# Natural-layout dO by a transposing DMA instead of TensorE, in a two-block attention backward kernel

## The chip, the cores and the metric

The kernel runs on one core of a Trainium2 chip. The metric is device time in microseconds (us) of the whole program: the median of three runs of the kernel before is 1736.88 us (1735.48 to 1741.37). A core has TensorE (PE; its weight loads stand apart as PEld), VectorE (DVE), ScalarE (ACT), GpSimd (POOL) and SyncE (SP), which does no arithmetic here and issues most DMAs. All DMAs run on the core's 16 DMA engines.

## The reference

Two attention blocks, A and B, each with its own x, cached K and V, wq and wo, work side by side; their outputs are concatenated. The kernel returns the forward output and the gradients of everything, for a given `grad_out`.

```python
B, Sq, D = 8, 96, 640
H, Sk, Dh = 32, 512, 128
def block(x, k_cache, v_cache, wq, wo):
    q = (x @ wq).reshape(B, Sq, H, Dh).transpose(0, 2, 1, 3)
    scores = einsum("bhqd,bhkd->bhqk", q, k_cache) * Dh ** -0.5
    p = softmax(scores)
    o = einsum("bhqk,bhkd->bhqd", p, v_cache)
    return o.transpose(0, 2, 1, 3).reshape(B, Sq, H * Dh) @ wo
out = concatenate([block(A...), block(B...)], axis=-1)
out, vjp = jax.vjp(f, ...);  grads = vjp(grad_out)     # all in bfloat16
```

So each block yields out (8x96x640), dx, dK and dV (8x32x512x128 each), dwq (640x4096) and dwo (4096x640). In each head, with g the block's half of `grad_out`: Q = x wq_h, dO = g wo_h^T, P = softmax(QK^T), dV = P^T dO, dP = dO V^T, dS = P (dP - rowsum(O dO)), dK = dS^T Q, dQ = dS K.

## The kernel before

**Unit of work.** An item is one head h and one batch b: 96 query rows against 512 keys. A block has 32 heads of 8 items, so there are 64 heads and 512 items in all. They run through a software pipeline in ticks: item (h, b) of the block that begins at tick0 enters at tick `tick0 + 8h + b`, and stage s of it is emitted at that tick plus `OFF[s]` (line 45): load at 0, transposes of K and V at 2 (`c_s1`), scores and softmax at 3, transposes of P at 4 and O^T at 5 (`c_s45`), dV at 4 (`c_s4`), dP, delta and dS at 6 (`c_s6`), transposes of dS and dK at 7 (`c_s7`, `c_s78`), dQ^T at 8. Within a tick the slots of `SLOTS` (line 50) set the order. Block B follows block A without a break. The framework's scheduler may still reorder by its own priorities; it inserts the waits and gives out the buffers of the tile pools (`bufs` of them for each name or tag).

**Work of a head.** `HK` (line 46) gives the ticks of what is done once a head, from the tick of its item b = 0:

- `pA` loads wq_h (POOL queue) and `pV` loads wo_h transposed, by a transposing DMA on SP's queue; `pB` takes the tiles QT_h and dOT_h.
- `pC` (line 192) makes Q^T and dO^T, each in two halves of four batches, by matmuls over the five 128-chunks of D, evicted by ScalarE or VectorE. Both have the head's 128 columns on partitions and the queries along the free dimension. QT_h is padded to 128 queries a batch, its pad set to zero by POOL (line 181); dOT_h is not padded.
- dK and dV need Q and dO the other way round, queries on partitions ("natural"). For Q this is `pN` (line 227): one transposing DMA of QT_h into Qnat_h, issued on SP at tick -1. For dO it is `pD` (line 213): eight TensorE transposes (line 223) in two halves, at ticks 2 and 7, and a VectorE copy of each half out of PSUM into dOnat_h (line 157, in `evac`).
- `pW` loads wq_h transposed (wqT_h, transposing DMA on SP, tick 2). `qA` (line 409) turns O^T and dQ^T into natural layout (Onat at tick 13, dQnat at 16), again by transposing DMAs on SP. `qB` and `qD` make dwo and dwq from them.
- So each head issues five transposing DMAs on SP: wo, wq, Q, O and dQ.

**Work of a group.** Out and dx are summed over groups of eight heads (`gU`, line 468): 24 more matmuls a head on average, spread over the 26 ticks after a group has ended. In the first eight heads there are none yet.

**Queues.** SP issues in one order, from one queue, each item's K and V load (lines 238 and 239), its dV and dK store (lines 340 and 406), 128 KB each, and the head's five transposes. A DMA instruction whose data or buffer isn't ready holds up all those behind it. POOL issues the loads of wq and wo rows and the stores of dwo, dwq and (block A) out and dx; it also scales P (line 295) and multiplies O by dO (line 349). K_sb has 11 buffers, V_sb 8, dK_sb and dV_sb 5 each, P_sb 5.

**Setup of a block.** x and g must be transposed for `pC`. Block A does it from its natural copies; block B, while A's last heads run, loads column chunks of 128 (`setup_ld`, line 91, ten DMAs on the POOL queue) and transposes each chunk on TensorE (`setup_cT`, line 100).

Of the kernel before, what the change touches and what calls it, by code (L numbers as in the profile page):

```python
# [8 lines left out]
ALU = mybir.AluOpType  # L9
AX = mybir.AxisListType  # L10
F32 = mybir.dt.float32
BF16 = mybir.dt.bfloat16
# [18 lines left out]
SL_LOAD = 0  # L31
# [9 lines left out]
SL_HEAD = 90  # L41
SL_GRP = 95
SL_SETUP = 96

OFF = dict(ld=0, s1=2, s2=3, s3=3, s4=4, s5=5, s6=6, s7=7, s8=8)
HK = dict(pA=-6, pB=-4, pV=-5, pW=2, pC0=[-3, -2], pC1=[0, 1], pD1=[2, 7], pN=-1, qA0=13, qA1=16, qB=[18, 19], qD=[(20, 0, 3), (23, 3, 5)])
# [6 lines left out]
def build_block(tc, em, tick0, blk, x, kc, vc, wq, wo, g_all, out_all, dx, dk, dv, dwq, dwo, ident, ones, pools, HG=8, first=True):  # L53
    nc = tc.nc
# [28 lines left out]
    def bank(shape, dt, name):  # L83
        return ps.tile(shape, dt, name=name, tag="bank")

    S = {}
# [1 line left out]
    HS = pools["HS"]  # L88
    CS = pools["CS"]

    def setup_ld(which_, c):
        def f():
            tmp = const.tile([128, TT, 128], BF16, name="ld_tmp", bufs=3)
            src_flat = x_flat if which_ == 0 else g_flat
            with nc.allow_non_contiguous_dma(reason="setup column chunk"):
                tc.keep_in_program_order(nc.gpsimd.dma_start(tmp[:], src_flat[:, c * 128:(c + 1) * 128].rearrange("(t p) d -> p t d", p=128)))
            S[("tmp", which_, c)] = tmp
        return f

    def setup_cT(which_, c):  # L100
        def f():
            key = "xT" if which_ == 0 else "gT"
            if c == 0:
                S[key] = const.tile([128, DC, T], BF16, name=key, bufs=1)
            tmp = S.pop(("tmp", which_, c))
            pt = bank([128, TT, 128], BF16, "tp_ps")
            for t in range(TT):
                nc.tensor.transpose(pt[:, t, :], tmp[:, t, :], ident[:])
            nc.vector.tensor_copy(S[key][:, c, :], pt[:].rearrange("p t d -> p (t d)"))
        return f  # L110

    def setup_T(which_, t):
# [21 lines left out]
    if first:  # L134
        assert TT % 2 == 0
        for t in range(TT):
            if t % 2 == 0:
                em.add(tick0 - 12, SL_LOAD, setup_nat(0, t, 2))
                em.add(tick0 - 11, SL_LOAD, setup_nat(1, t, 2))
            em.add(tick0 - 10 + t // 2, SL_SETUP, setup_T(0, t))  # L140
            em.add(tick0 - 7 + t // 2, SL_SETUP, setup_T(1, t))
    else:
        for c in range(DC):
            em.add(tick0 - 12 + c + (c >= 3), SL_LOAD, setup_ld(0, c))
            em.add(tick0 - 9 + c, SL_SETUP, setup_cT(0, c))
            em.add(tick0 - 7 + c, SL_SETUP + 1, setup_ld(1, c))
            em.add(tick0 - 5 + c, SL_SETUP, setup_cT(1, c))
    if not first:
        em.add(tick0 + B + OFF["s5"] - 2, SL_LOAD, setup_nat(1))
        em.add(tick0 + B + OFF["s8"] - 2, SL_LOAD, setup_nat(0))  # L150
# [26 lines left out]
    def pB(h):  # L177
        def f():
            st = HS[(blk, h)]
            st["QT_h"] = hd.tile([128, B, 128], BF16, name="QT_h")  # L180
            nc.gpsimd.memset(st["QT_h"][:, :, Sq:128], 0.0)
            st["dOT_h"] = hd.tile([128, T], BF16, name="dOT_h")
        return f

    def pW(h):
# [6 lines left out]
    def pC(h, which, si):  # L192
        def f():
            st = HS[(blk, h)]
            (t0, w) = tsplits[si]
            b0 = t0 // Sq
            if which == 0:
                dst = st["QT_h"][:, b0:b0 + w // Sq, 0:Sq]
                lhs = lambda c: st["wq_h"][:, c, :]
                rhsT = S["xT"]  # L200
                sc = scale
            else:
                dst = st["dOT_h"][:, t0:t0 + w].rearrange("p (b q) -> p b q", q=Sq)
                lhs = lambda c: st["woT_h"][:, c, :]
                rhsT = S["gT"]
                sc = None
            q_ps = bank([128, w], F32, "q_ps")
            for c in range(DC):
                nc.tensor.matmul(q_ps[:], lhs(c), rhsT[:, c, t0:t0 + w], start=(c == 0), stop=(c == DC - 1))  # L209
            evac(EV["pC%d%d" % (which, si)], dst, q_ps[:].rearrange("p (b q) -> p b q", q=Sq), sc)  # L210
        return f

    def pD(h, half):
        def f():
            st = HS[(blk, h)]
            if half == 0:
                st["dOnat_h"] = hd.tile([Sq, B * 128], BF16, name="dOnat_h")
            b0 = half * HB
            nb = B - b0 if half else HB
            n_ps = bank([Sq, 8 * 128], BF16, "n_ps")  # L220
            for i in range(nb):
                b = b0 + i
                nc.tensor.transpose(n_ps[:, i * 128:(i + 1) * 128], st["dOT_h"][:, b * Sq:(b + 1) * Sq], ident[:])  # L223
            evac("dve", st["dOnat_h"][:, b0 * 128:(b0 + nb) * 128], n_ps[:, 0:nb * 128])
        return f

    def pN(h):
        def f():
            st = HS[(blk, h)]
            st["Qnat_h"] = hd.tile([128, B, 128], BF16, name="Qnat_h")  # L230
            tc.keep_in_program_order(nc.sync.dma_start_transpose(st["Qnat_h"][:], st["QT_h"][:].rearrange("p b q -> p (b q)")))
        return f

    def c_ld(h, b):
# [95 lines left out]
    def c_s4(h, b):  # L330
        def f():
            st = CS[(blk, h, b)]
            hs = HS[(blk, h)]
            P_sb = st["P_sb"]
            dV_ps = bank([128, KC * 128], F32, "dV_ps")
            for c in range(KC):
                nc.tensor.matmul(dV_ps[:, c * 128:(c + 1) * 128], P_sb[:, c * 128:(c + 1) * 128], hs["dOnat_h"][:, b * 128:(b + 1) * 128], start=True, stop=True)  # L337
            dV_sb = wk.tile([128, KC * 128], BF16, name="dV_sb", bufs=5)
            nc.scalar.activation(dV_sb[:], dV_ps[:], ACT.Identity, scale=1.0)  # L339
            nc.sync.dma_start(dv[b, h].rearrange("(p c) d -> p (c d)", c=KC), dV_sb[:])  # L340
        return f

    def c_s5b(h, b):
        def f():
            st = CS[(blk, h, b)]
            hs = HS[(blk, h)]
            tok = slice(b * Sq, (b + 1) * Sq)
            prod = wk.tile([128, Sq], BF16, name="prod", bufs=3)
            nc.gpsimd.tensor_tensor(prod[:], hs["OT_h"][:, tok], hs["dOT_h"][:, tok], op=ALU.mult)  # L349
            st["prod"] = prod  # L350
        return f

    def c_s6(h, b):
        def f():
            st = CS[(blk, h, b)]
            hs = HS[(blk, h)]
            tok = slice(b * Sq, (b + 1) * Sq)
            dP_ps = bank([Sq, Sk], F32, "dP_ps")
            nc.tensor.matmul(dP_ps[:], hs["dOT_h"][:, tok], st["VT"], start=True, stop=True)  # L359
# [58 lines left out]
    def qB(h, di):  # L418
        def f():
            st = HS[(blk, h)]  # L420
            Onat = st["Onat"]
            if "dwo_sb" not in st:
                st["dwo_sb"] = hd.tile([128, D], BF16, name="dwo_sb")
                st["dwo_n"] = 0
            dwo_sb = st["dwo_sb"]
            (c0, w) = dsplits[di]
# [9 lines left out]
    def qD(h, c_lo, c_hi):  # L436
        def f():
            st = HS[(blk, h)]
            dQnat = st["dQnat"]
            if "dwq_sb" not in st:  # L440
                st["dwq_sb"] = hd.tile([128, DC, 128], BF16, name="dwq_sb")
                st["dwq_n"] = 0
            dwq_sb = st["dwq_sb"]
            ncn = c_hi - c_lo
# [1 line left out]
            for ci in range(ncn):  # L446
                c = c_lo + ci
                for t in range(TT):
                    nc.tensor.matmul(w_ps[:, ci * 128:(ci + 1) * 128], S["x_nat"][:, t, c * 128:(c + 1) * 128], dQnat[:, t, :],  # L449
                                     start=(t == 0), stop=(t == TT - 1))  # L450
            evac("act" if ncn > 1 else "dve", dwq_sb[:, c_lo:c_hi, :].rearrange("p a b -> p (a b)"), w_ps[:, 0:ncn * 128])
            st["dwq_n"] += ncn
            if st["dwq_n"] == DC:
                with nc.allow_non_contiguous_dma(reason="per-head dwq slice"):
                    nc.gpsimd.dma_start(dwq_v[:, :, h * 128:(h + 1) * 128], dwq_sb[:])
        return f

    def gW(g, hh):
# [38 lines left out]
    for h in range(H):  # L497
# [1 line left out]
        em.add(c0t + HK["pA"], SL_LOAD, pA(h))  # L499
        em.add(c0t + HK["pB"], SL_HEAD, pB(h))  # L500
        em.add(c0t + HK["pV"], SL_HEAD, pV(h))
        em.add(c0t + HK["pN"], SL_HEAD + 0.5, pN(h))
        em.add(c0t + HK["pW"], SL_HEAD, pW(h))
        for si in range(NTS):
            em.add(c0t + HK["pC0"][min(si, len(HK["pC0"]) - 1)], SL_HEAD, pC(h, 0, si))
            em.add(c0t + HK["pC1"][min(si, len(HK["pC1"]) - 1)], SL_HEAD, pC(h, 1, si))
        for half in range(2):
            em.add(c0t + HK["pD1"][half], SL_HEAD, pD(h, half))
        for b in range(B):
            ct = c0t + b  # L510
            em.add(ct + OFF["ld"], SLOTS["LOAD"], c_ld(h, b))
# [142 lines left out]
```

## Time and profile before

One execution was profiled: 1739.57 us, of which its span (first to last recorded instruction) is 1737.8 us. The engine rows count arithmetic only; DMA-issuing instructions are not counted as busy, so SP has no such row and its load must be read from the timeline of its queue.

| view | before |
|---|---|
| span / time of the profiled run | 1737.8 / 1739.57 us |
| TensorE clock granted | 1.00 |
| DMA moved | 387.46 MB, mean 223 GB/s |
| DMA packets under 512 B | 294560 of 573454 |
| HBM read / written | 161.09 / 159.12 MB |
| SP's issues | 2079 copies, 320 transposes |
| copies dV, dK, K, V | 512 each, 128 KB, 3.2 to 3.4 us to landing |
| transposes Qnat_h, Onat, dQnat | 64 each, 4.5, 4.2 and 3.7 us to landing |
| transposes woT_h, wqT_h | 64 each, 3.7 to 3.8 us to landing |
| POOL memset of QT_h | 64 of 311 ns |

How to read it: times are us unless marked ns. A group's row gives line, engine, operation and tile (out<-in), then total busy time and mean length of one, then the engine's idle time just before. Matmuls are pipelined: the length of one (219 ns for 128 columns) is not the distance to the next (56 ns). A wait's row reads: who waited, for whom, us in total, how often, longest. A row of a time window gives its bounds, its length, the busy time and count on PE, PEld, DVE, ACT and POOL, then the granted clock, the DMA engines' busy share and GB/s. A row of a queue's timeline gives start, length, and what was issued.

### The profile page before, as it was taken

Reading aid. Unit: us, or ns where it says so; the run is one execution under the profiler, and the core shown is the slowest. Engines: PE = TensorE matmul, PEld = TensorE weight load, DVE = VectorE, ACT = ScalarE, POOL = GpSimd, SP = SyncE. Lnnn points to the kernel's source line nnn. Section 1 sums busy time; section 2 is a strip of 40 time slices with the busy share of each in tenths; the row PEclk is TensorE's granted clock in tenths of the full one; section 3 lists DMA queues with packets and bytes.
Section 4 is the critical chain, followed back from the end, with each engine's and each line's share of the span. In section 5 each row is a group of like instructions: output and inputs, shape, how many; then the busy total and the mean of one; then the engine's idle time right before and its main releaser. Section 6 shows DMA issues by size and latency. Waiting matters only on the chain.

```text
span 1737.8 us, 64947 instructions
## 1 busy us (share of the span) xinstructions
PE 1717.4 (99%) x24056; PEld 1441.5 (83%) x24056; DVE 1410.6 (81%) x2943; ACT 1476.5 (85%) x4081; POOL 767.5 (44%) x1385
## 2 busy tenths in 40 slices
PE   8999999999999999999999999999999999999998
PEld 6877888888888888888888888888888888888886
DVE  7877777888888888888887888778888888888885
ACT  6988888988889888888777999888888888888883
POOL 3444433444434444445455544344443444444441
PEclk9999999999999999999999999999999999999999
DMA  9998999989899988899999989999899989888994
GB/s 226 219 226 222 226 230 215 231 231 221 224 215 222 224 227 213 218 228 235 250 241 247 231 224 224 225 222 228 232 223 212 213 228 228 223 217 224 230 218 123
DMA packets 573454, 387.46 MB, mean 223 GB/s; under 512 B 294560, under 2 KB 561696, under 8 KB 573136
## 3 DMA queue, kind: packets, MB, share of 16 engines
q1 hardware_dynamic: 556656, 335.62, 80.3%
q0 software_dynamic: 16480, 47.70, 10.4%
q8 instruction: 188, 3.08, 0.8%
q14 instruction: 130, 1.06, 0.3%
HBM read 161.09 MB, written 159.12 MB: 184 GB/s over the span
## 4 chain that ended last, share of the span: by engine, by line
PE 96%; DMA 2%; DVE 0%; ACT 0%; issue 0%; POOL 0%; SPq 0%; DVEq 0%; POOLq 0%; ACTq 0%
PE q_ps L209 12%; PE o_ps L483 12%; PE kvT_ps L250 6%; PE dK_ps L403 6%; PE dV_ps L337 6%; PE kvT_ps L248 6%; PE dP_ps L359 6%; PE S_ps L264 6%; PE dwq_ps L449 6%; PE dwo_ps L429 6%; PE dq_dst_ps L386 5%; PE optp_ps L320 5%; PE optp_ps L311 5%; PE dq_dst_ps L377 5%; PE n_ps L223 2%; DMA woT_h<-in_A_wo_dram 1%
## 5 line engine op out<-in xcount | busy, mean ns | idle before, releaser
L295 POOL TENSOR_SCALAR P_sb<-E_sb,rinv 96x512 bf16<-96x512 bf16 x512 | 352.2, 688 | 638.5 <-DVE rinv L286 635.2
L363 DVE SCALAR_TENSOR_TENSOR dS_sb<-dP_ps,dl_ps,P_sb 96x512 bf16<-96x512 f32 x512 | 384.7, 751 | 102.1 <-PE dl_ps L361 88.3
L276 ACT ACTIVATE E_sb<-S_ps,negm 96x512 bf16<-96x512 f32 x512 | 348.6, 681 | 124.5 <-DVE negm L266 124.0
L266 DVE TENSOR_REDUCE negm<-S_ps 96x1 f32<-96x512 f32 x512 | 348.2, 680 | 68.3 <-PE S_ps L264 67.7
L252 DVE COPY KVT<-kvT_ps 128x1024 bf16<-128x1024 bf16 x512 | 349.4, 682 | 41.1 <-PE kvT_ps L250 24.2
L405 ACT ACTIVATE dK_sb<-dK_ps 128x512 bf16<-128x512 f32 x512 | 301.6, 589 | 56.4 <-PE dK_ps L403 53.2
L339 ACT ACTIVATE dV_sb<-dV_ps 128x512 bf16<-128x512 f32 x512 | 316.0, 617 | 0.0
L326 ACT ACTIVATE PT_sb<-optp_ps 128x384 bf16<-128x384 bf16 x512 | 254.7, 497 | 0.0
L349 POOL TENSOR_TENSOR prod<-OT_h,dOT_h 128x96 bf16<-128x96 bf16 x512 | 186.9, 365 | 106.5 <-ACT OT_h L323 87.6
L250 PE MATMUL kvT_ps<-ident,V_sb 128*128 128x128 bf16 x2048 | 197.9, 219 | 2.0 <-DMA V_sb<-in_A_v_cache_dram 2.0
L248 PE MATMUL kvT_ps<-ident,K_sb 128*128 128x128 bf16 x2048 | 197.9, 219 | 0.8 <-DMA K_sb<-in_A_k_cache_dram 0.8
L337 PE MATMUL dV_ps<-dOnat_h,P_sb 96*128 96x128 bf16 x2048 | 197.9, 219 | 0.0
L403 PE MATMUL dK_ps<-Qnat_h,dS_sb 96*128 96x128 bf16 x2048 | 197.9, 219 | 0.0
L264 PE MATMUL S_ps<-KVT,QT_h 128*96 128x512 bf16 x512 | 193.7, 378 | 1.6 <-DVE KVT L252 1.5
L359 PE MATMUL dP_ps<-KVT,dOT_h 128*96 128x512 bf16 x512 | 195.2, 381 | 0.0
L248 PEld LDWEIGHTS <-K_sb 128*128 128x128 bf16 x2048 | 152.9, 98 | 41.9 <-issue 1.7
L388 DVE COPY dST_sb<-dq_dst_ps 128x384 bf16<-128x384 bf16 x512 | 178.9, 349 | 2.9 <-PE dq_dst_ps L386 1.8
L386 PE MATMUL dq_dst_ps<-ident,dS_sb 96*128 96x96 bf16 x2048 | 172.1, 206 | 1.1 <-DVE dS_sb L363 1.0
L320 PE MATMUL optp_ps<-ident,P_sb 96*128 96x96 bf16 x2048 | 171.6, 205 | 1.5 <-POOL P_sb L295 1.5
L311 PE MATMUL optp_ps<-PT_sb,V_sb 128*128 128x96 bf16 x2048 | 172.1, 206 | 0.0
L377 PE MATMUL dq_dst_ps<-dST_sb,K_sb 128*128 128x96 bf16 x2048 | 170.8, 206 | 0.0
L449 PE MATMUL dwq_ps<-dQnat,x_nat 128*128 128x128 bf16 x1920 | 142.6, 219 | 3.5 <-DMA dQnat<-dQT_h 3.3
(70 smaller groups left out, 3475.0 us busy)
## 6 DMA issues: line engine op xcount, KB each, us to landing
out_dram<-dV_sb SPq DMA_DIRECT2D x512, 128.0 KB, 3.3
out_dram<-dK_sb SPq DMA_DIRECT2D x512, 128.0 KB, 3.2
K_sb<-in_A_k_cache_dram SPq DMA_DIRECT2D x256, 128.0 KB, 3.4
V_sb<-in_A_v_cache_dram SPq DMA_DIRECT2D x256, 128.0 KB, 3.4
K_sb<-in_B_k_cache_dram SPq DMA_DIRECT2D x256, 128.0 KB, 3.4
V_sb<-in_B_v_cache_dram SPq DMA_DIRECT2D x256, 128.0 KB, 3.3
out_dram<-dwo_sb POOLq DMA_DIRECT2D x64, 160.0 KB, 3.5
out_dram<-dwq_sb POOLq DMA_DIRECT2D x64, 160.0 KB, 4.6
```

The costliest lines, as they stand in the source:

```text
L248: nc.tensor.transpose(kvT_ps[:, c * 128:(c + 1) * 128], st["K_sb"][:, c, :], ident[:])
L250: nc.tensor.transpose(kvT_ps[:, Sk + c * 128:Sk + (c + 1) * 128], st["V_sb"][:, c, :], ident[:])
L252: nc.vector.tensor_copy(KVT[:], kvT_ps[:])
L266: nc.vector.tensor_reduce(negm[:], S_ps[:], axis=AX.X, op=ALU.max, negate=True)
L276: nc.scalar.activation(E_sb[:], st["S_ps"][:], ACT.Exp, bias=st["negm"][:], scale=1.0, accum_out=rowsum[:])
L295: nc.gpsimd.tensor_scalar(P_sb[:], st["E_sb"][:], st["rinv"][:], 0.0, op0=ALU.mult, op1=ALU.add)
L337: nc.tensor.matmul(dV_ps[:, c * 128:(c + 1) * 128], P_sb[:, c * 128:(c + 1) * 128], hs["dOnat_h"][:, b * 128:(b + 1) * 128], start=True, s ...
L339: nc.scalar.activation(dV_sb[:], dV_ps[:], ACT.Identity, scale=1.0)
L359: nc.tensor.matmul(dP_ps[:], hs["dOT_h"][:, tok], st["VT"], start=True, stop=True)
L363: nc.vector.scalar_tensor_tensor(dS_sb[:], dP_ps[:], dl_ps[:, 0:1], st["P_sb"][:], op0=ALU.subtract, op1=ALU.mult)
L403: nc.tensor.matmul(dK_ps[:, c * 128:(c + 1) * 128], dS_sb[:, c * 128:(c + 1) * 128], hs["Qnat_h"][0:Sq, b, :], start=True, stop=True)
L405: nc.scalar.activation(dK_sb[:], dK_ps[:], ACT.Identity, scale=1.0)
```

## The change

Natural dO now comes, like natural Q, from a transposing DMA on SP's queue, but only from the ninth head of block A on and in all of block B; in the first eight heads of block A both natural Q and natural dO are made by TensorE transposes. For this dOT_h takes QT_h's padded form and its pad is set to zero by POOL. dV moves from the item's tick 4 to its tick 6 (transposes of P stay at 4). The wqT transpose moves from tick 2 to 6 of the head, that of O from 13 to 12. Block B loads its x and g by six row chunks each (1280 contiguous bytes a row) instead of five column chunks (256 bytes). The row tiles, dwo_sb and dwq_sb share six buffers (before: 3, 2 and 2), and dV_sb has six buffers instead of five. Qnat_h and dOnat_h now have the same shape.

```diff
-OFF = dict(ld=0, s1=2, s2=3, s3=3, s4=4, s5=5, s6=6, s7=7, s8=8)
-HK = dict(pA=-6, pB=-4, pV=-5, pW=2, pC0=[-3, -2], pC1=[0, 1], pD1=[2, 7], pN=-1, qA0=13, qA1=16, ...)
+OFF = dict(ld=0, s1=2, s2=3, s3=3, s4=4, sv=6, s5=5, s6=6, s7=7, s8=8)
+HK = dict(pA=-6, pB=-4, pV=-5, pW=6, pC0=[-3, -2], pC1=[0, 1], pD1=[2, 7], pD0=[3, 6], pN=[-1, 1], qA0=12, qA1=16, ...)
...
+    def row640(name):
+        return hd.tile([128, D], BF16, name=name, tag="row640", bufs=6)
+
-    def setup_ld(which_, c):
-            tmp = const.tile([128, TT, 128], BF16, name="ld_tmp", bufs=3)
-            ... nc.gpsimd.dma_start(tmp[:], src_flat[:, c * 128:(c + 1) * 128].rearrange("(t p) d -> p t d", p=128))
+    def setup_ld(which_, t):
+            tmp = row640("ld_tmp")
+            ... nc.gpsimd.dma_start(tmp[:], src_flat[t * 128:(t + 1) * 128, :])
...
-            pt = bank([128, TT, 128], BF16, "tp_ps")
-            for t in range(TT):
-                nc.tensor.transpose(pt[:, t, :], tmp[:, t, :], ident[:])
-            nc.vector.tensor_copy(S[key][:, c, :], pt[:].rearrange("p t d -> p (t d)"))
+            pt = bank([128, DC, 128], BF16, "tp_ps")
+            for c in range(DC):
+                nc.tensor.transpose(pt[:, c, :], tmp[:, c * 128:(c + 1) * 128], ident[:])
+            nc.vector.tensor_copy(S[key][:, :, t * 128:(t + 1) * 128], pt[:])
...
-        for c in range(DC):
-            em.add(tick0 - 12 + c + (c >= 3), SL_LOAD, setup_ld(0, c))
-            em.add(tick0 - 9 + c, SL_SETUP, setup_cT(0, c))
-            em.add(tick0 - 7 + c, SL_SETUP + 1, setup_ld(1, c))
-            em.add(tick0 - 5 + c, SL_SETUP, setup_cT(1, c))
+        for t in range(TT):
+            em.add(tick0 - 11 + t, SL_LOAD, setup_ld(0, t))
+            em.add(tick0 - 9 + t, SL_SETUP, setup_cT(0, t))
+            em.add(tick0 - 8 + t, SL_LOAD, setup_ld(1, t))
+            em.add(tick0 - 6 + t, SL_SETUP, setup_cT(1, t))
...
     def pB(h):
-            nc.gpsimd.memset(st["QT_h"][:, :, Sq:128], 0.0)
-            st["dOT_h"] = hd.tile([128, T], BF16, name="dOT_h")
+            st["dOT_h"] = hd.tile([128, B, 128], BF16, name="dOT_h")
+            for k in range(2):
+                if BYDMA[k](h):
+                    nc.gpsimd.memset(st["dOT_h" if k else "QT_h"][:, :, Sq:128], 0.0)
...
-    def pD(h, half):
+    BYDMA = [lambda h: not first or h >= 8, lambda h: not first or h >= 8]
+    def pD(h, which, half):
...
+            src = st["dOT_h" if which else "QT_h"]
+            name = "dOnat_h" if which else "Qnat_h"
...
-                nc.tensor.transpose(n_ps[:, i * 128:(i + 1) * 128], st["dOT_h"][:, b * Sq:(b + 1) * Sq], ident[:])
+                nc.tensor.transpose(n_ps[:, i * 128:(i + 1) * 128], src[:, b0 + i, 0:Sq], ident[:])
...
-    def pN(h):
+    def pN(h, which):
...
+            src = st["dOT_h" if which else "QT_h"]
+            name = "dOnat_h" if which else "Qnat_h"
+            st[name] = hd.tile([128, B, 128], BF16, name=name)
+            tc.keep_in_program_order(nc.sync.dma_start_transpose(st[name][:], src[:].rearrange("p b q -> p (b q)")))
...
-            dV_sb = wk.tile([128, KC * 128], BF16, name="dV_sb", bufs=5)
+            dV_sb = wk.tile([128, KC * 128], BF16, name="dV_sb", bufs=6)
...
-                st["dwo_sb"] = hd.tile([128, D], BF16, name="dwo_sb")
+                st["dwo_sb"] = row640("dwo_sb")
...
-                st["dwq_sb"] = hd.tile([128, DC, 128], BF16, name="dwq_sb")
+                st["dwq_sb"] = row640("dwq_sb")
...
-        em.add(c0t + HK["pN"], SL_HEAD + 0.5, pN(h))
+        for k in range(2):
+            if BYDMA[k](h):
+                em.add(c0t + HK["pN"][k], SL_HEAD + 0.5, pN(h, k))
...
         for half in range(2):
-            em.add(c0t + HK["pD1"][half], SL_HEAD, pD(h, half))
+            for k in range(2):
+                if not BYDMA[k](h):
+                    em.add(c0t + HK["pD1" if k else "pD0"][half], SL_HEAD, pD(h, k, half))
...
-            em.add(ct + OFF["s4"], SLOTS["S4"], c_s4(h, b))
+            em.add(ct + OFF["sv"], SLOTS["S4"], c_s4(h, b))
```

More of the change, by code (lines that the diff above doesn't have):

```diff
@@ L43 @@
 SL_SETUP = 96
-OFF = dict(ld=0, s1=2, s2=3, s3=3, s4=4, s5=5, s6=6, s7=7, s8=8)
-HK = dict(pA=-6, pB=-4, pV=-5, pW=2, pC0=[-3, -2], pC1=[0, 1], pD1=[2, 7], pN=-1, qA0=13, qA1=16, qB=[18, 19], qD=[(20, 0, 3), (23, 3, 5)])
+OFF = dict(ld=0, s1=2, s2=3, s3=3, s4=4, sv=6, s5=5, s6=6, s7=7, s8=8)
+HK = dict(pA=-6, pB=-4, pV=-5, pW=6, pC0=[-3, -2], pC1=[0, 1], pD1=[2, 7], pD0=[3, 6], pN=[-1, 1], qA0=12, qA1=16, qB=[18, 19], qD=[(20, 0, 3), (23, 3, 5)])
 EV = dict(pB0="act", pB1="dve", pC00="act", pC01="act", pC10="act", pC11="dve", pD0="dve", pD1="dve", qA0="dve", qA1="dve", qB0="act", qB1="act", gU="act")
@@ L89, in build_block, with setup_cT @@
     CS = pools["CS"]
-    def setup_ld(which_, c):
+    def row640(name):
+        return hd.tile([128, D], BF16, name=name, tag="row640", bufs=6)
+    def setup_ld(which_, t):
         def f():
-            tmp = const.tile([128, TT, 128], BF16, name="ld_tmp", bufs=3)
+            tmp = row640("ld_tmp")
             src_flat = x_flat if which_ == 0 else g_flat
-            with nc.allow_non_contiguous_dma(reason="setup column chunk"):
-                tc.keep_in_program_order(nc.gpsimd.dma_start(tmp[:], src_flat[:, c * 128:(c + 1) * 128].rearrange("(t p) d -> p t d", p=128)))
-            S[("tmp", which_, c)] = tmp
+            tc.keep_in_program_order(nc.gpsimd.dma_start(tmp[:], src_flat[t * 128:(t + 1) * 128, :]))
+            S[("tmp", which_, t)] = tmp
         return f
-    def setup_cT(which_, c):
+    def setup_cT(which_, t):
         def f():
             key = "xT" if which_ == 0 else "gT"
-            if c == 0:
+            if t == 0:
                 S[key] = const.tile([128, DC, T], BF16, name=key, bufs=1)
-            tmp = S.pop(("tmp", which_, c))
-            pt = bank([128, TT, 128], BF16, "tp_ps")
-            for t in range(TT):
-                nc.tensor.transpose(pt[:, t, :], tmp[:, t, :], ident[:])
-            nc.vector.tensor_copy(S[key][:, c, :], pt[:].rearrange("p t d -> p (t d)"))
+            tmp = S.pop(("tmp", which_, t))
+            pt = bank([128, DC, 128], BF16, "tp_ps")
+            for c in range(DC):
+                nc.tensor.transpose(pt[:, c, :], tmp[:, c * 128:(c + 1) * 128], ident[:])
+            nc.vector.tensor_copy(S[key][:, :, t * 128:(t + 1) * 128], pt[:])
         return f
@@ L202, in f @@
             else:
-                dst = st["dOT_h"][:, t0:t0 + w].rearrange("p (b q) -> p b q", q=Sq)
+                dst = st["dOT_h"][:, b0:b0 + w // Sq, 0:Sq]
                 lhs = lambda c: st["woT_h"][:, c, :]
@@ L211, in pC @@
         return f
-    def pD(h, half):
+    BYDMA = [lambda h: not first or h >= 8, lambda h: not first or h >= 8]
+    def pD(h, which, half):
         def f():
             st = HS[(blk, h)]
+            src = st["dOT_h" if which else "QT_h"]
+            name = "dOnat_h" if which else "Qnat_h"
             if half == 0:
-                st["dOnat_h"] = hd.tile([Sq, B * 128], BF16, name="dOnat_h")
+                st[name] = hd.tile([128, B, 128], BF16, name=name)
             b0 = half * HB
@@ L221, in f @@
             for i in range(nb):
-                b = b0 + i
-                nc.tensor.transpose(n_ps[:, i * 128:(i + 1) * 128], st["dOT_h"][:, b * Sq:(b + 1) * Sq], ident[:])
-            evac("dve", st["dOnat_h"][:, b0 * 128:(b0 + nb) * 128], n_ps[:, 0:nb * 128])
+                nc.tensor.transpose(n_ps[:, i * 128:(i + 1) * 128], src[:, b0 + i, 0:Sq], ident[:])
+            evac("dve", st[name][0:Sq, b0:b0 + nb, :].rearrange("p b d -> p (b d)"), n_ps[:, 0:nb * 128])
         return f
-    def pN(h):
+    def pN(h, which):
         def f():
             st = HS[(blk, h)]
-            st["Qnat_h"] = hd.tile([128, B, 128], BF16, name="Qnat_h")
-            tc.keep_in_program_order(nc.sync.dma_start_transpose(st["Qnat_h"][:], st["QT_h"][:].rearrange("p b q -> p (b q)")))
+            src = st["dOT_h" if which else "QT_h"]
+            name = "dOnat_h" if which else "Qnat_h"
+            st[name] = hd.tile([128, B, 128], BF16, name=name)
+            tc.keep_in_program_order(nc.sync.dma_start_transpose(st[name][:], src[:].rearrange("p b q -> p (b q)")))
         return f
@@ L336, in f @@
             for c in range(KC):
-                nc.tensor.matmul(dV_ps[:, c * 128:(c + 1) * 128], P_sb[:, c * 128:(c + 1) * 128], hs["dOnat_h"][:, b * 128:(b + 1) * 128], start=True, stop=True)
-            dV_sb = wk.tile([128, KC * 128], BF16, name="dV_sb", bufs=5)
+                nc.tensor.matmul(dV_ps[:, c * 128:(c + 1) * 128], P_sb[:, c * 128:(c + 1) * 128], hs["dOnat_h"][0:Sq, b, :], start=True, stop=True)
+            dV_sb = wk.tile([128, KC * 128], BF16, name="dV_sb", bufs=6)
             nc.scalar.activation(dV_sb[:], dV_ps[:], ACT.Identity, scale=1.0)
@@ L348, in f @@
             prod = wk.tile([128, Sq], BF16, name="prod", bufs=3)
-            nc.gpsimd.tensor_tensor(prod[:], hs["OT_h"][:, tok], hs["dOT_h"][:, tok], op=ALU.mult)
+            nc.gpsimd.tensor_tensor(prod[:], hs["OT_h"][:, tok], hs["dOT_h"][:, b, 0:Sq], op=ALU.mult)
             st["prod"] = prod
@@ L358, in f @@
             dP_ps = bank([Sq, Sk], F32, "dP_ps")
-            nc.tensor.matmul(dP_ps[:], hs["dOT_h"][:, tok], st["VT"], start=True, stop=True)
+            nc.tensor.matmul(dP_ps[:], hs["dOT_h"][:, b, 0:Sq], st["VT"], start=True, stop=True)
             dl_ps = bank([Sq, 1], F32, "dl_ps")
@@ L450, in f @@
                                      start=(t == 0), stop=(t == TT - 1))
-            evac("act" if ncn > 1 else "dve", dwq_sb[:, c_lo:c_hi, :].rearrange("p a b -> p (a b)"), w_ps[:, 0:ncn * 128])
+            evac("act" if ncn > 1 else "dve", dwq_sb[:, c_lo * 128:c_hi * 128], w_ps[:, 0:ncn * 128])
             st["dwq_n"] += ncn
@@ L454, in f @@
                 with nc.allow_non_contiguous_dma(reason="per-head dwq slice"):
-                    nc.gpsimd.dma_start(dwq_v[:, :, h * 128:(h + 1) * 128], dwq_sb[:])
+                    nc.gpsimd.dma_start(dwq_v[:, :, h * 128:(h + 1) * 128], dwq_sb[:].rearrange("p (c d) -> p c d", d=128))
         return f
```

## The prediction

> **What bounds the kernel now.** The first view is the page: busy shares, DMA queues, the chain that ended last.
>
> ```profile
> PE 1717.4 (99%) x24056; PEld 1441.5 (83%) x24056; DVE 1410.6 (81%) x2943; ACT 1476.5 (85%) x4081; POOL 767.5 (44%) x1385
> ...
> q1 hardware_dynamic: 556656, 335.62, 80.3%
> ...
> PE 96%; DMA 2%; DVE 0%; ACT 0%; issue 0%; POOL 0%; SPq 0%; DVEq 0%; POOLq 0%; ACTq 0%
> ```
>
> PE carries the chain, and the engine rows have no entry for SP, which issues all of q1. DMA holds 2% of the chain, so the next view is where PE waited: its waits of the first eight heads (25 to 220 us), then busy time in a stretch there and in one for the rest.
>
> ```profile
> PE dwq_ps L449 <- DMA dQnat<-dQT_h: 3.3, 2, 2.4
> PE kvT_ps L250 <- DMA V_sb<-in_A_v_cache_dram: 2.0, 3, 0.9
> PE q_ps L209 <- DMA woT_h<-in_A_wo_dram: 1.9, 3, 1.3
> ```
>
> ```profile
> 101.00:181.00 80.00, 75.38 (x1084) 63.24 (x1083) 62.93 (x130) 70.96 (x198) 36.55 (x67) 1.00 0.94 231
> 260.00:1670.00 1410.00, 1410.00 (x19851) 1187.11 (x19849) 1162.27 (x2424) 1217.37 (x3364) 638.33 (x1147) 1.00 0.93 226
> ```
>
> From 260 to 1670 us PE is busy 1410 of 1410 us and waits for nothing. From 101 to 181 us (heads 4 to 6 from 0, whose group sums have not begun) it has less work, 75.4 of 80 us, and waits for transfers at a granted clock of 1.00. So **two paces** stand close together, and the early stretch shows the second: SP's queue. Its timeline there:
>
> ```profile
> 143.05 0.38 SPq L340 DMA_DIRECT2D out_dram<-dV_sb  x1
> 143.48 1.27 SPq L173 DMA_TRANSPOSE woT_h<-in_A_wo_dram  x1
> 144.85 1.69 SPq L238 DMA_DIRECT2D K_sb<-in_A_k_cache_dram  x1
> 146.63 0.38 SPq L239 DMA_DIRECT2D V_sb<-in_A_v_cache_dram  x1
> 147.10 0.38 SPq L406 DMA_DIRECT2D out_dram<-dK_sb  x1
> 147.58 1.23 SPq L415 DMA_TRANSPOSE Onat<-OT_h  x1
> 148.90 0.54 SPq L340 DMA_DIRECT2D out_dram<-dV_sb  x1
> 149.53 0.38 SPq L238 DMA_DIRECT2D K_sb<-in_A_k_cache_dram  x1
> ```
>
> One issue follows another with 0.1 us between: a copy 0.38, a transpose 1.2 to 1.3, the copy behind a transpose 0.53, and every nine us or so one that takes 1 to 2 us. Counted over that timeline:
> - 101 to 181 us, PE waiting: 97 copies and 15 transposes, that is 26.4 us for one head's 32 copies and five transposes.
> - 208 to 480 us: 335 copies and 52 transposes, 26.0 us a head. SP is late throughout but catching up: around 210 us its issues start 8 to 13 us after the buffer came free or the eviction ended that they need, around 490 us 0 to 3 us after.
> - Over the whole run that lateness has a median of 5.6 us, and idle gaps over 0.1 us on SP add to 65 us, some 20 of them in the tail.
>
> PE's pace from head 8 to the last is 1490.2 us (first K transpose at 208.5, last at 1698.7) over 56 heads, 26.6 us. SP needs 26.0 to 26.4. The kernel is PE-bound with 0.2 to 0.6 us a head to spare on SP.
>
> **The change, part by part.**
>
> *dO from TensorE to DMA, heads 8 to 63.* The group rows:
>
> ```profile
> L157 DVE COPY dOnat_h<-n_ps 96x512 bf16<-96x512 bf16 x128 | 52.5, 410 | 0.0
> L223 PE MATMUL n_ps<-ident,dOT_h 128*96 128x128 bf16 x512 | 52.1, 223 | 0.0
> ```
>
> The 223 ns is a pipelined length; start to start these transposes take 61 ns (31.4 us over 512, the chain's 2%). Eight a head leave 56 heads: 448 x 0.0614 = 27.5 us of PE, 0.49 a head, so PE's pace becomes 26.1. Also 112 VectorE copies of 0.41 us go, beside PE's work: no gain. SP gets 56 transposes of 1024 columns. The nearest row is Qnat_h, the same shape from a tile with the same padding: issue 1.30 us at the median, 4.5 us to landing. Its slot on SP is 1.30, plus 0.10 of gap, plus 0.15 by which the next copy is longer: 1.55. A straight line through SP's counts in groups of five (60 to 470, 545 to 840, 980 to 1570 us) gives 0.58 a copy and 1.59 a transpose, which agrees. Ends: 0.53, if it were one more copy slot (0.48 mean and a gap; less is excluded, since it is an added issue); 2.02, if the 16 DMA engines and not the issue are what fills (1024 packets of 256 B at their mean of 31.6 ns, over 16). I take 1.55, the row of the same shape. SP then needs 26.0 + 1.55 = 27.55 us a head and PE 26.1: **SP sets the pace**.
>
> *First eight heads.* Eight Qnat transposes leave SP, which sets the pace there: 26.4 - 1.55 = 24.85 us a head. PE gains 64 transposes, 0.49 a head, on 75.4/3 = 25.1: 25.6. Heads 3 to 7 run at 25.0 to 27.5 now; taking 1 us for each of five, **-5 us**. If PE's cover were gone this would cost up to 64 x 0.0614 = 3.9 us. The 16 new VectorE copies, 6.6 us, fit into VectorE's idle 17 of 80 us.
>
> *Moves.* dV goes from tick 4 to 6: same matmuls, eviction and store, only later in SP's order. P_sb is read at tick 6 by dS anyway. The new wait is dV's on dOnat_h: issued at tick 1, needed at 6, 5 x 3.3 = 16.5 us, less 1.3 issue, 4.5 landing and SP's lateness of 5.6: 5 us over. At a lateness over 10.7 it is late, about where K loads are (issue to use has a median of 7.8, landing takes 3.4). Queued behind a late dV on PE are dP, and ScalarE's eviction. So when SP falls behind, PE waits for K, V or dOnat, at SP's pace and not beyond it. The wqT transpose (tick 2 to 6) and Onat (13 to 12) spread the six; their sum stays. SP's waits for the dOT and OT evictions are covered by its own lateness.
>
> *POOL and block B.* 48 more memsets of 0.31 us, 15 us on an engine busy 44%, with P_sb and prod behind them: covered; uncovered, 15 us. Rows for x and g: 12 issues of 160 KB (as wo_r, 0.59 us) for 10 of 0.86, and 1280 B runs for 256 B. They lie in heads 31 to 34, which take PE 29 to 30 us: nothing either way.
>
> **Sum.** 56 x 27.55 = 1542.8 us for heads 8 to 63. SP may fall some 8 us behind before PE waits (PE waited early at lateness of 9 to 14, against 3 to 5 on entering head 8 once the first heads are lighter): 1534.8, against 1490.2, +44.6; with the first heads -5, **+39.6**. The profiled run took 1739.57 (span 1737.8, so 1.8 lies around it): 1779.2. The median of the runs shown, 1736.88, is 2.7 lower: 1776.5, forecast 1776.
>
> **Rivals.**
>
> *SP has room after all, PE stays the bound* (faster). By place: SP's issues hold about 4.4 us a head over their floors (0.38 and 1.22). If that excess were only waiting that shrinks when the queue is pressed, SP would need as little as 26.0 - 4.4 + 1.55 = 23.15 us, less than PE's 26.1. It decides at a total of 26.6. Time: -27.5 - 5 gives 1707 profiled, 1704. For it: 260 to 1670 us without one PE wait, and slices that moved up to 250 GB/s against a mean of 223. Against it: from 101 to 181 us the queue was pressed, PE waited, and the excess was 4.4 to 5.2 us a head. Chance 0.15.
>
> The Trainium skill, Perfetto Trace Analysis, Identifying the Most-Contended Engine, would judge PE by its weight loads, not by matmul busy time: 83% here, so that taking work off PE frees less than 27.5 us and this rival ends between 1704 and 1732. The starts in this trace leave no gap, so I hold to the larger gain.
>
> *A transpose costs little*: 0.53, one copy slot, up to 1.16, two fitted copies for its 256 KB: 26.5 to 27.2 us a head. At 0.53, 56 x 26.53 - 8 - 1490.2 - 5 = -17.5: 1719; at 1.16, +17.8: 1755. For it: a transpose's issue might overlap the engines' backlog. Against: its issue alone, 1.30, is longer than two copies, and the copy behind it is slower, not faster. Chance 0.12, a third each for faster, same, slower.
>
> The Trainium skill, Advanced Engine Details and Errata, X-Bar Transpose (TRN2), states that transposing DMAs are as fast as regular ones; that is this rival's upper end, 1755. On this trace the issue rows speak against it.
>
> *The DMA engines fill first*: 2.02 a transpose, 28.02 a head, +65.9: 1803; with 26.4 as base, 1825. For it: DMA share 0.93 to 0.94 already. Chance 0.2 to come out over 1790, 0.05 over 1806.
>
> *The change does not do what it says*, the scheduler putting the transpose where SP waits for VectorE: SP's lateness of 5.6 us hides such a wait; within the forecast.
>
> **Numbers.** Forecast case and its dearer form 0.73 (1755 to 1825; the likeliest one's own range 1757 to 1806), cheap transpose 0.12, PE-bound 0.15. Faster by over 0.3%, about what a measurement of this kernel can tell from no change: 0.15 + 0.04 = 0.19, and 0.01 for the unlisted, 0.20. Same: 0.04 and 0.01, 0.05. Slower: 0.75. The range leaves out the PE-bound case and what is over 1806, 0.2 together: 1718 to 1806.
>
> **What would show it.** Right: in 260 to 1670 us PE is busy under 97% and waits for K_sb, V_sb, dOnat_h, dQnat or woT_h; SP has no idle gaps and needs 27 to 28 us a head; Qnat_h and dOnat_h issues take 1.3 us; n_ps counts 128; heads 3 to 7 are about 1 us shorter. Wrong: PE busy all through at 26.1 us a head, with SP's long issues fewer; or PE held by P_sb or dS instead of transfers, or the clock granted under 1.00.

## The result, and the profile after

The changed kernel takes 1791.45 us (median of four runs, 1781.58 to 1793.36) against 1739.12 us of the kernel before in the same comparison: ratio 1.029, interval [1.025, 1.034]. The forecast was 1776 with a range of 1718 to 1806. The profiled run took 1789.58 us, span 1787.8.

The page of the changed kernel, the rows shown of before:

```profile
PE 1715.7 (96%) x23672; PEld 1427.2 (80%) x23672; DVE 1380.8 (77%) x2849; ACT 1474.4 (82%) x4081; POOL 775.0 (43%) x1435
...
q1 hardware_dynamic: 607344, 348.21, 81.9%
...
PE 81%; DMA 15%; ACT 1%; DVE 1%; issue 1%; POOL 0%; SPq 0%; DVEq 0%; ACTq 0%; POOLq 0%
```

PE has 384 matmuls less and a span that is 50 us longer. In the chain DMA went from 2% to 15%. The two time windows (columns as before):

```profile
101.00:181.00 80.00, 80.00 (x1174) 68.26 (x1172) 68.46 (x144) 74.61 (x208) 36.82 (x66) 1.00 0.96 234
260.00:1670.00 1410.00, 1352.06 (x18669) 1123.34 (x18667) 1085.01 (x2232) 1169.93 (x3237) 624.25 (x1158) 0.99 0.95 226
```

The two stretches have changed places. In the first eight heads PE is now busy 80 of 80 us; from 260 to 1670 us it has lost 58 of 1410, at a granted clock of 0.99. PE's six longest waits in that long stretch, where before there was none:

```profile
PE dwq_ps L458 <- DMA dQnat<-dQT_h: 25.6, 16, 3.5
PE q_ps L213 <- DMA woT_h<-in_B_wo_dram: 10.0, 7, 2.1
PE dV_ps L346 <- DMA dOnat_h<-dOT_h: 8.5, 10, 1.8
PE q_ps L213 <- DMA woT_h<-in_A_wo_dram: 2.7, 4, 1.2
PE kvT_ps L259 <- DMA V_sb<-in_B_v_cache_dram: 2.6, 6, 0.7
PE kvT_ps L257 <- DMA K_sb<-in_B_k_cache_dram: 1.9, 4, 0.9
```

All six are for transfers that SP issues, of five kinds, and the new one is only third. With K and V of block A, transfers hold 54.4 of the 58 us. SP's timeline around one of the added transposes:

```profile
1211.09 0.39 SPq L247 DMA_DIRECT2D K_sb<-in_B_k_cache_dram  x1
1211.59 2.45 SPq L240 DMA_TRANSPOSE dOnat_h<-dOT_h  x1
1214.13 1.15 SPq L415 DMA_DIRECT2D out_dram<-dK_sb  x1
1215.37 0.38 SPq L248 DMA_DIRECT2D V_sb<-in_B_v_cache_dram  x1
```

No gap beyond the usual 0.1 us, and here two of the long issues fall together. The rows of TensorE's remaining dO and Q transposes count 64 each, 128 together, and the added DMA has this entry in the view of its tile:

```profile
L240 SPq DMA_TRANSPOSE dOnat_h<-dOT_h x56: 1237/1304/2618, 209.0 to 1736.2; - x56
```

Four measures, read the same way in every run below: **SP's pace** is the time for one head's 32 K, V, dK and dV copies between 260 and 1670 us, with all that lies between; **PE's pace** is the distance of first to last K transpose from the ninth head on, over 56; **lateness** is how long after its buffer came free a K load is issued; **SP's idle time** is the sum of the gaps over 0.15 us between its issues, 260 to 1650 us.

| | before | after |
|---|---|---|
| SP's pace, us a head | 26.6 (held back by PE) | 27.7 |
| PE's pace, us a head | 26.6 | 27.55 |
| lateness, median | 5.6 | 10.3 |
| SP's idle time, us of 1390 | 36 | 20 |
| heads 3 to 7, us each | 25.0, 26.6, 26.7, 26.7, 27.5 | 23.8, 24.4, 26.0, 25.5, 26.0 |

### The profile page after: what moved, and what is told of

Its sections match the earlier page's. It is cut to its first block, busy times and chain, and to the rows that moved or that the text cites. A ratio compares the mean times of both kernels' runs of the same rounds, so it can differ in the third digit from the quotient of the medians.

```text
span 1787.8 us, 64313 instructions
## 1 busy us (share of the span) xinstructions
PE 1715.7 (96%) x23672; PEld 1427.2 (80%) x23672; DVE 1380.8 (77%) x2849; ACT 1474.4 (82%) x4081; POOL 775.0 (43%) x1435
## 2 busy tenths in 40 slices
DMA packets 624077, 400.02 MB, mean 224 GB/s; under 512 B 345280, under 2 KB 612416, under 8 KB 623760
## 4 chain that ended last, share of the span: by engine, by line
PE 81%; DMA 15%; ACT 1%; DVE 1%; issue 1%; POOL 0%; SPq 0%; DVEq 0%; ACTq 0%; POOLq 0%
PE q_ps L213 11%; PE o_ps L492 10%; PE kvT_ps L259 6%; PE kvT_ps L257 6%; PE dV_ps L346 5%; PE dK_ps L412 5%; PE dwo_ps L438 5%; PE S_ps L273 5%; PE dP_ps L368 5%; PE dwq_ps L458 5%; PE dq_dst_ps L395 4%; PE dq_dst_ps L386 4%; PE optp_ps L320 4%; PE optp_ps L329 4%; DMA dQnat<-dQT_h 4%; DMA dOnat_h<-dOT_h 3%
## 5 line engine op out<-in xcount | busy, mean ns | idle before, releaser
L259 PE MATMUL kvT_ps<-ident,V_sb 128*128 128x128 bf16 x2048 | 199.4, 220 | 4.0 <-DMA V_sb<-in_B_v_cache_dram 2.6
L458 PE MATMUL dwq_ps<-dQnat,x_nat 128*128 128x128 bf16 x1920 | 143.6, 220 | 28.4 <-DMA dQnat<-dQT_h 26.7
```

Source lines behind the costliest of these rows:

```text
L259: nc.tensor.transpose(kvT_ps[:, Sk + c * 128:Sk + (c + 1) * 128], st["V_sb"][:, c, :], ident[:])
```

## The experiments

The theories, before any of these ran. **S**: SP's queue sets the pace; each issue takes its own time there, and the added transpose is one issue too many. **D**: the same, but the 16 DMA engines are what is full. **L**: single transfers land late for their reader, above all dOnat_h for dV. Eleven kernels were run. All ratios are to the kernel before, with their 95% intervals.

| run | us | ratio | PE's pace | SP idle, us |
|---|---|---|---|---|
| e1 all but the main step | 1734.56 | 0.998 [0.997, 0.999] | 26.6 | 52 |
| e2 the added DMA alone, unread | 1786.27 | 1.028 [1.026, 1.031] | 27.5 | 25 |
| e3 neither DMA nor TensorE | 1709.50 | 0.984 [0.982, 0.985] | 26.1 | 26 |
| e4 after, half of dK stores on POOL | 1710.46 | 0.984 [0.983, 0.986] | 26.1 | 41 |
| e5 after, stores of half the bytes | 1754.38 | 1.011 [1.008, 1.013] | 27.05 | 19 |
| e6 after, dwq two ticks later | 1797.16 | 1.033 [1.029, 1.037] | 27.7 | 25 |
| e7 after, half of dK stores on ScalarE | 1804.24 | 1.040 [1.037, 1.042] | 27.8 | 125 |
| e8 before, half of dK stores on POOL | 1729.27 | 0.996 [0.994, 0.997] | 26.6 | 188 |
| e9 after, a plain copy for the transpose | 1741.99 | 1.002 [1.000, 1.004] | 26.8 | 28 |
| e10 after, dO by DMA in every second head | 1742.62 | 1.002 [1.000, 1.005] | 26.8 | 35 |
| e11 all by DMA, most dK stores on POOL | 1710.72 | 0.983 [0.981, 0.985] | 26.2 | 105 |

### The step apart from the rest (e1, e2, e3)

```diff
-    BYDMA = [lambda h: not first or h >= 8, lambda h: not first or h >= 8]
+    BYDMA = [lambda h: not first or h >= 8, lambda h: False]
```

> All of the change except its main step: natural dO stays on TensorE in every head. Theory S (SP's queue sets the pace, 0.53 us for a copy and about 1.6 us for a transpose; the added transpose is the loss): SP is back at 26.0 to 26.4 us a head, PE at 26.6 from the ninth head on, and the first heads keep their gain of 3 to 5 us: 1732 to 1737 us. Theory D (the same, but the 16 DMA engines are what is full, not SP's issue) expects the same here. If a side part costs something (dV at the sixth tick, x and g by rows, shared buffers), over 1742 us.

1734.56 us, as expected. PE is busy 1390 of 1390 us from 260 to 1650. So dV at the sixth tick, rows for x and g, the shifted transposes and the shared buffers cost nothing that shows; the first eight heads, 5.2 us shorter in the trace, give the 4 us.

e2 adds to e1 the transposing DMA into a tile of its own (`dOdum_h`), from the ninth head on:

```diff
-            name = "dOnat_h" if which else "Qnat_h"
-            st[name] = hd.tile([128, B, 128], BF16, name=name)
+            name = "dOdum_h" if which else "Qnat_h"
+            st[name] = hd.tile([128, B, 128], BF16, name=name, bufs=1 if which else 2)
```

> TensorE makes natural dO in every head, and from the ninth head on the transposing DMA is issued as well, into a tile that nothing reads: the DMA's cost alone, without PE's gain and without anybody waiting for its result. The tile needs room, so dV_sb and the row tiles have five buffers each. Theories S and D: SP needs 27.6 to 27.8 us a head against PE's 26.6, so 1780 to 1800 us, as the changed kernel. Theory L (the loss is that dOnat_h lands late for dV, so that dV stands on PE and all behind it): nobody waits for this tile, 1732 to 1742 us.

1786.27 us, and SP's pace is 27.7. The waits went to dQnat (10.2 us), K and V. **L falls**: nobody reads the tile. And PE does 0.49 us a head more than in the changed kernel (the estimate of the prediction), at no more time: PE's gain is worth nothing there.

e3 is the changed kernel with POOL writing a constant where the DMA wrote dO:

```diff
-            tc.keep_in_program_order(nc.sync.dma_start_transpose(st[name][:], src[:].rearrange("p b q -> p (b q)")))
+            if which:
+                nc.gpsimd.memset(st[name][:], 0.5)
+            else:
+                tc.keep_in_program_order(nc.sync.dma_start_transpose(st[name][:], src[:].rearrange("p b q -> p (b q)")))
```

> The changed kernel without the transposing DMA: from the ninth head on a POOL memset writes a constant to dOnat_h, so natural dO is left out of the computation there and dV is not the reference's. It shows what taking the 448 transposes off PE is worth when nothing takes their place. Theories S and D: PE needs 26.1 us a head, SP 26.0 to 26.4; 1705 to 1725 us. If PE were not the bound before, or its gaps swallowed the gain, 1730 to 1740 us.

1709.50 us. Against e1 that is 25.1 us for the 448 transposes taken off PE, where the prediction had 27.5. So the two halves of the step, measured apart: the removal is worth -25, the DMA without the removal costs +52 (e2 less e1; one buffer fewer for dV_sb and the row tiles is in it), and both together +57 (after less e1), not the sum. That 57 is more than 52 lies within the scatter of the changed kernel (1782 to 1793). They do not add, because SP's queue sets the pace as soon as it is the longer one.

SP's occupied time a head, its pace less its idle time (260 to 1650 us), shows the price in the queue itself: 25.55 in e1 and 27.13 in e2, 25.75 in e3 and 27.30 in the changed kernel, so 1.58 and 1.55 for the one transpose.

### SP's issue or the DMA engines (e4, e5, e9)

e4 moves every second dK store to POOL's queue:

```diff
-            nc.sync.dma_start(dk[b, h].rearrange("(p c) d -> p (c d)", c=KC), dK_sb[:])
+            (nc.gpsimd if b % 2 else nc.sync).dma_start(dk[b, h].rearrange("(p c) d -> p (c d)", c=KC), dK_sb[:])
```

> The changed kernel with the dK store of every second item issued from POOL's queue instead of SP's: the same bytes on the same 16 DMA engines, four issues a head fewer on SP. Theory S: SP needs 27.7 - 4 x 0.53 = 25.6 us a head, PE's 26.1 is the bound again: 1705 to 1725 us. Theory D: the engines have as much to do as before, 1780 to 1800 us. A result between tells of both.

1710.46 us, as fast as e3, where dO is not transposed at all. Its window, and all waits on PE in that stretch:

```profile
260.00:1650.00 1390.00, 1388.22 (x19456) 1163.48 (x19454) 1131.46 (x2326) 1212.54 (x3370) 768.23 (x1417) 1.00 1.03 239
```

```profile
PE dV_ps L346 <- DMA dOnat_h<-dOT_h: 0.9, 1, 0.9
PE dwq_ps L458 <- DMA dQnat<-dQT_h: 0.8, 2, 0.6
```

The same bytes pass, 400.0 MB, at 239 GB/s, and the engines' busy share went up, to 1.03, while PE stopped waiting. **D falls** as the bound: a share of 0.95 in the changed kernel was not full. POOL's stores go in larger packets, so there are 4% fewer of them (599500 against 624077), but the packets' time did not fall: 0.95 of 27.7 us is 26.3 us a head, 1.03 of 26.15 is 26.9. Nor was SP held by stores whose data was not ready: it had stood idle for 20 us in all of 1390. POOL pays 0.594 us for each of 256 issues, in time that it had.

The Trainium skill, DMA: Bandwidth & Descriptors, Rules for kernel authors, says that spreading DMAs over SP, ScalarE and GpSimd gives no bandwidth and saves only the sequencer's issue time. The second half holds here: the issue time was what was short, and saving it was worth 81 us. The first half is not tested: 239 GB/s are the same bytes in less time.

e5 goes the other way, the same issues with fewer bytes:

```diff
-            nc.sync.dma_start(dk[b, h].rearrange("(p c) d -> p (c d)", c=KC), dK_sb[:])
+            nc.sync.dma_start(dk[b, h].rearrange("(p c) d -> p (c d)", c=KC)[:, 0:256], dK_sb[:, 0:256])
```

(and the same for dV)

> The changed kernel with every dK and dV store cut to half of its columns (128 rows of 512 bytes instead of 1024), so half of dK and dV is left out of the output; number and order of the issues stay. Theory S: SP's 0.38 us a copy hang on the issue and not on the bytes; the pace stays near 27.6 us a head, 1775 to 1795 us. Theory D: one MB less a head on the 16 engines, of 6.2, is more than the transpose brought; PE's 26.1 is the bound again, 1705 to 1725 us. Between the two if the long issues (1 to 2 us) come from full engines.

1754.38 us, between the two expectations, nearer to S (the profiled run took 1760).

```profile
260.00:1650.00 1390.00, 1353.56 (x18755) 1128.40 (x18753) 1090.09 (x2243) 1173.18 (x3253) 628.51 (x1163) 0.99 0.83 192
```

The engines' share fell from 0.95 to 0.83, and SP's pace only from 27.7 to 27.3: of what one MB a head less could free, 0.45 us came back. A copy's issue has the same median (0.38) with half the bytes; the gain is in the tails (a transpose 1.36 us for 1.41 at the mean). So the issue time is for the most part the issue's own, and a smaller part goes with what the transfers have to move. That smaller part is 37 us of the kernel's time, nearly half of what e4 won: with two paces this close, 0.45 us a head counts. Lack of room in the queue does not make the issues long: in e8 below, where SP stands idle for 188 of 1390 us, their medians are 0.38 (copy) and 1.28 (transpose), against 0.39 and 1.26 in the changed kernel.

e9 puts a plain copy in the place of the added transpose:

```diff
-            tc.keep_in_program_order(nc.sync.dma_start_transpose(st[name][:], src[:].rearrange("p b q -> p (b q)")))
+            if which:
+                tc.keep_in_program_order(nc.sync.dma_start(st[name][:], src[:]))
...
```

> The changed kernel with a plain copy of dOT_h into dOnat_h in place of the added transpose: the same 256 KB from SBUF to SBUF and the same waits, but 128 rows of 2 KB instead of 1024 pieces of 256 bytes; dO is not turned, so dV is not the reference's from the ninth head on. Theory S: the price is SP's issue, 0.53 us for a copy; SP needs 26.5 to 26.9 us a head and PE 26.1: 1715 to 1740 us. Theory D by bytes: as dear as the transpose, 1780 to 1795 us.

1741.99 us, 2 us over S's range and 38 us under D's by bytes. SP needs 27.0 us a head; the added copy, the only one of SP's with 2 KB rows and the only one from SBUF to SBUF, is issued in 0.50 us (median), not 0.38. e9 does not exclude a D that counts packets' time: 128 packets of 2 KB at their mean of 91 ns are 12 us of one engine, 1024 of 256 bytes at 30 ns are 30. That form of D is excluded by e4.

### Where the crossing lies (e10), and whether a late transfer costs by itself (e6)

e10 transposes dO by DMA in every second head:

```diff
+    BYDMA = [lambda h: not first or h >= 8, lambda h: (not first or h >= 8) and h % 2 == 1]
```

> The changed kernel with dO transposed by DMA only in every second head from the ninth on, by TensorE in the others: 28 added transposes instead of 56. Theory S: SP needs on average 26.0 to 26.3 + 0.8 = 26.8 to 27.1 us a head, PE 26.35; with 8 us of lateness that PE bears, 1735 to 1755 us. If the loss grew evenly with each transpose (no crossing from PE-bound to SP-bound), half of the changed kernel's loss, 1763 us.

1742.62 us: inside S's range, and not at half the loss. SP's pace is 26.97. With 27.71 for all heads, half a transpose a head is 0.74 us, so one is **1.48 us**, and on a straight line none leaves **26.2**. With a share f of the heads by DMA, SP would need 26.2 + 1.48 f and PE 26.6 - 0.49 f: an estimate by which they cross at f = 0.2, one head in five; no run has that share. The runs of this kernel scatter more than the others, 1732 to 1756.

e6 reads dQnat two ticks later:

```diff
-HK = dict(..., qD=[(20, 0, 3), (23, 3, 5)])
+HK = dict(..., qD=[(22, 0, 3), (25, 3, 5)])
```

> The changed kernel with dwq's two parts two ticks later (22 and 25 for 20 and 23), so that the largest wait on PE, 26.7 us for dQnat, has seven us more. Theory S: the waits only show where PE meets SP's lateness; they move to other transfers and the time stays, 1780 to 1797 us. Theory L (each late transfer costs by itself): the dQnat waits go and nothing comes for them, 1760 to 1768 us.

1797.16 us, the upper end of S's range. The dQnat waits are down to 0.8 us, and K came in their place (the longest three of the list on PE, 260 to 1650 us):

```profile
PE kvT_ps L257 <- DMA K_sb<-in_A_k_cache_dram: 10.9, 10, 2.4
PE kvT_ps L257 <- DMA K_sb<-in_B_k_cache_dram: 10.8, 8, 2.2
PE q_ps L213 <- DMA woT_h<-in_A_wo_dram: 5.7, 6, 2.6
```

So the longest wait in the list was not a cause. It named the transfer with the least slack.

### Other queues (e7, e8, e11)

e7 is e4 with `nc.scalar` in the place of `nc.gpsimd`.

> As the run with stores on POOL's queue, but from ScalarE's: its queue uses the same packets as SP's. Theory S: SP is relieved by 2.1 us a head and PE is the bound, 1705 to 1725 us, if an issue on ScalarE costs what it costs on SP, 0.4 to 0.5 us (ScalarE is busy some 83% and has 4 us a head). Theory D: no gain, 1780 to 1800 us. If long issues of 1 to 2 us strike ScalarE as they strike SP, its evictions come late: 1725 to 1760 us.

1804.24 us, worse than all three expectations. ScalarE's issues are short (0.34 us, the longest 0.40), so the long issues were not the reason. ScalarE's own waits:

```profile
ACT dQT_h L401 <- DMA V_sb<-in_B_v_cache_dram: 19.7, 11, 3.7
ACT dQT_h L401 <- DMA out_dram<-dV_sb: 18.2, 3, 10.0
...
ACT OT_h L332 <- DMA out_dram<-dV_sb: 14.0, 7, 3.1
```

These evictions do not read V_sb or wait for a dV store. In the trace the eight completion semaphores of SP's DMAs count ScalarE's as well (261 to 288 of SP's and 18 to 45 of ScalarE's on each); before its own DMA ScalarE waits on the one that it will use, and so for earlier transfers of SP. That ties ScalarE to SP's transfers, and PE to ScalarE (PE waits 18.8 us for dQT_h and 16.2 for PT_sb). POOL's DMAs have eight of their own. SP's queue is not the bound in e7: it is occupied for 25.4 us a head, stands idle for 125 us, and the median lateness of K loads is 1.9 us against 10.3 in the changed kernel. So S's relief of SP came and its time did not, for a wait that no theory had. That this sharing is the whole loss was not tried apart.

e8 makes the same edit as e4 to the kernel before.

> The kernel before with the dK store of every second item on POOL's queue: SP relieved where PE is the bound. Theory S: from the ninth head on PE keeps 26.6 us a head, nothing gained there; in heads 3 to 7 SP was the pace, some 5 to 8 us go: 1729 to 1736 us. If moving stores off SP were worth something by itself, 1705 to 1720 us.

1729.27 us. The ninth head now begins at 199.4 us instead of 208.5; from there to the last 1489.1 us against 1490.2. Relief for SP is worth something only where SP is the bound.

e11 takes e4 further: `BYDMA` is true for all heads, and `b % 4` sends three of four dK stores to POOL.

> Natural Q and dO by DMA in all heads, the first eight too, and three of four dK stores on POOL's queue. Theory S: SP needs 27.7 - 6 x 0.53 = 24.5 us a head, less than PE's 26.1 from the ninth head on and about PE's own in the first eight, and PE loses the last 128 transposes, 8 us: 1702 to 1710 us, no slower than the run with every second store on POOL. If POOL's issues, 0.6 to 0.9 us each, make P_sb and prod late: 1715 to 1740 us.

1710.72 us, the time of e4, 0.7 over the expectation: the forecast gain of 8 us did not come. PE's pace is 26.2, and SP stands idle for 105 us, so more relief for SP has nothing left to win. Heads 3 to 7 are uneven (22.9 to 28.9 us), and from head 0 to head 8 the kernel takes 189.2 us against 189.9 in e4, though PE has 128 transposes less there; what holds those heads was not looked into. e4 and e11 are the fastest kernels here that compute everything, 1.6 to 1.7% under before.

## Why the prediction was right, by its steps

**What bounds the kernel** was right: two paces close together, PE's 26.6 and SP's 26.0 to 26.4 us a head. e10 and the changed kernel give 26.2 for SP without the added transpose, e3 and e4 give PE 26.1 without the TensorE transposes, as forecast.

**The price of a transpose** was forecast as 1.55 us; the runs give 1.48 (e10 against the changed kernel) to 1.58 (e1 against e2). Of the two ends, the copy slot of 0.53 was added up wrongly: its terms, 0.48 and a gap of 0.10, make 0.58, which moves that rival's time by 3 us and no verdict. e9 shows that a plain copy of the same bytes costs 27.0 - 26.2 = 0.8, and e4 that the other end, the engines' packet time, does not bind.

**The sum** came 10 us short of the profiled run (1779.2 against 1789.6). Heads 8 to 63 took 1542.9 us, forecast 1534.8: SP's pace was 27.71 and not 27.55. By e10's line the base of 26.0, read where the queue caught up, was 0.2 low. The 8 us that PE bears before it waits came out as 56 x 27.71 - 1542.9 = 9. Head 0 began 1.9 us later in this run (between 12.7 and 15.2 in the other runs, whatever the kernel). The first heads gave 5.2 us from head 0 to head 8, forecast 5.

**The moves** cost nothing, as forecast (e1). The wait of dV for dOnat_h appears (8.5 us, 10 times) and is not the price: e2 has the price without it. The 7.8 us that the prediction has from a K load's issue to its use are too few: over the whole run before, the median is 10.2. In the changed kernel dQnat and woT_h, not K, head the list of waits.

**The signs** came as named, but for one: the prediction counted a clock under 1.00 as a sign of being wrong, and it was 0.99. The trace has it at one half in five records of 3.4 us each, 17 us of the 1410; that takes at most 8.5 us from PE, in a stretch in which PE stood still for 58, and SP, which set the pace, stood idle for only 20 us, so it can have waited little for a slower PE.

**The rivals.** "SP has room after all" asked for an excess that shrinks when the queue is pressed. It did not: issues over the floors of 0.38 and 1.22 us took 285 us in the changed kernel and 281 before. "A transpose costs little", the Trainium skill's rule on X-bar transposes (Advanced Engine Details and Errata, X-Bar Transpose (TRN2)), put the time at 1755; the added 256 KB transposed cost 57 us over e1, the same 256 KB copied plainly 7 us. From issue to landing the two are closer, 3.7 and 3.1 us; the trace disagrees with that rule where SP's issue is what counts, 1.30 us against 0.50. "The DMA engines fill first" gave 1803, a little closer to 1791 than the forecast of 1776, yet it is not what happened: e4 moves the same bytes in 1710.

## What to carry to other kernels

An engine that only issues has no busy row, so count its queue from its timeline: issues a unit of work times their own lengths, against the unit's time on the busy engine. Work moved off the bound engine onto a queue with less room than the work needs is a loss of the difference, even if the work is as small as one transpose a head; the lists of waits then name whichever transfer has the least slack, and moving that one moves the wait. Before paying for room with other work, look for a queue that stands idle: four stores a head on POOL turned a 2.9% loss into a 1.6% gain. And measure it: the same stores on ScalarE took 94 us longer than on POOL.

## What the runs showed of the hardware that was not expected

- **Long issues and instruction fetch.** Of 148 issues in the changed kernel that took over half a microsecond more than their kind (260 to 1650 us), 134 lie within 1.5 us of a 16 KB packet of the instruction queue; at random times 45% would. There were 144 such packets, of 1.23 us each, one every 9.6 us, and the long issues held 147 us beyond the floors, a tenth of SP's time. The counts are about the same before (142 of 155) and with half the bytes (137 of 147). Whether the fetch is what makes these issues long was not tried apart.
- **A busy share over 1.** In e4 the DMA engines' share was 1.03 with PE short of data for 1.7 us of 1390, so packet times overlap in part and a share of 0.95 says little of room.
- **The copy behind a transpose** takes 0.53 us instead of 0.38, in all runs.
